# Sliding-window attention with channel mix, one core: another order of the same operations

## The chip, the cores and the metric

The kernel runs on one core of a Trainium2 chip. The metric is the device time of one execution in microseconds. Engines are named as in the profile: PE is TensorE, PEld its weight loads, DVE VectorE, ACT ScalarE, POOL GpSimd, SP SyncE. POOL and SP do almost nothing but start transfers.

## What is computed

Attention over 8 batches and 8 heads of 576 positions and 64 columns, with a window of 128 positions and a linear bias, and behind it a channel mix in which every position is mixed with the one before it:

```python
scores = scale * np.matmul(q, k.transpose(0, 1, 3, 2))
bias = slopes[:, None, None] * (-np.abs(rel).astype(np.float32))[None, :, :]
mask = (rel >= 0) & (rel < window)
scores = np.where(mask, scores + bias[None], -1000000000.0)
attn = softmax(scores)
x = np.matmul(attn, v)              # heads side by side: 8 x 576 x 512
xk = mu_k * x + (1.0 - mu_k) * x_prev
xr = mu_r * x + (1.0 - mu_r) * x_prev
k = np.maximum(xk @ w_k, 0.0)       # 512 to 1024
v = k * k @ w_v                     # 1024 to 512
out = v / (1.0 + np.exp(-(xr @ w_r)))
```

Inputs and output are float32; inside, the kernel works in bfloat16 and sums in float32.

## The kernel before

**Attention.** The work is cut into 32 pairs of heads, numbered 0 to 31; pair 4b+g is heads 2g and 2g+1 of batch b. For each pair there is a chain of operations, with these names: `tr` and `tl` (DVE transposes q and k, the large part and the tail of 64 positions, L179 and L187), `sh` (SP moves a part of q to other partitions, `qt<-qt`, L195), `score` (PE, L241 and L246, into two score banks), `exp` (ACT, L262), `mask` (DVE multiplies by the bias as a factor, L270), `av` (PE, L286, again into a score bank), `rc` and `norm` (DVE, L297 and L301, which read that bank and write xu), and then the transposition of the result. For batches 0 to 3 PE transposes (`ot`, L310) and ACT copies (`xt`, L321). For batches 4 to 7 a crossbar transpose started from SP does it (`xt` too, L315, `xt<-xu`). Batch 0 goes another way ahead of its scores: PE transposes q and k (`tq`, `tk`, `tail`), ACT and DVE copy (`pq`, `pk`, `tcopy`), and each pair is done in two parts, so that names there have a last number 0 or 1.

**Mix.** `dl` (DVE, L335) takes the difference to the position before; it is the first reader of what the transpose wrote. `ma` and `mr` scale it for the two mixes (ACT, L342, or DVE, L344), `xk` (DVE, L354) adds.

**Feed-forward.** Two batches together are a batch pair P, 0 to 3, cut into units of 256 to 512 positions. `m1.P.c.f` (PE, L366) multiplies a unit that begins at position c by a block f of w_k (in the first two blocks its first three matmuls are called `m1a`); `rl` (ACT, L372) and `kk` (ACT, L379, or DVE, L381) are the ReLU and the square; `m3` (PE, L388) and `rs` (ACT, L394) are the gate; `m2a` and `m2` (PE, L403) are the two halves of the product with w_v for 128 positions; `oo` (DVE, L410) multiplies gate and product, `st` (SP, L415) stores. In the last piece, `3.4`, `m2a`, `m2`, `oo` and `st` are done in two halves of 256 columns.

**Loads.** POOL starts them: `lql`, `lqp`, `lts` (q and k), `lvs` (v; `lvs.b.4` is its tail), `lwk`, `lwr`, `lwv` (weights). `clear.b` are DVE memsets of the places of v that no load fills (tv and vs of batch b, L487 to L489); the first `lvs` of a batch waits for it. Others at the start: `fill` (PE multiplies zeros), `sid`, `dper`, `dcopy`, `mask0`, `mcopy` (bias tables), `ms` (memsets), `c` (casts of the first q and k), `clrk`, `id8`, `tmu`, `cmu`.

**Buffers.** Four PSUM banks for matrix work ("mm"), two double banks for scores and `av` ("sa"), three buffers each for xu, the differences (mb) and rl, two for kk.

**What sets the order.** Each engine runs its instructions strictly in the order of the program. A table `ORDER` in the kernel names, for PE, ACT, DVE, POOL and SP, every operation in the order in which that engine is to run it. A loop `plan` then writes the program: it takes from each engine's list only the operation that the table has next and issues it when those that it depends on are written; its cost numbers only decide how the engines' lists are interleaved. Waits between engines follow from the data. The table has one more use: a square or a scaling whose name stands in ACT's list runs on ACT, else on DVE.

```python
for text in ORDER.values():
    line = [tuple(int(x) if x.isdigit() else x for x in w.split(".")) for w in text.split()]
    for a, o in zip(line, line[1:]):
        ops[o]["after"] = [a]
plan()
```

Of the kernel before, what the change touches and what calls it, by code (L numbers as in the profile page):

```python
# [16 lines left out]
def kernel(  # L17
# [473 lines left out]
    def clear_first():  # L491
# [5 lines left out]
            fill.8 fill.5 tq.0 fill.12 fill.6 fill.4 fill.7 fill.2 tmu tk.0 tk.3 tq.3  # L497
            tk.2 tq.2 score.0.0 score.3.0 fill.13 tail.0 tq.1 score.2.0 tk.1 fill.11
            score.3.1 av.3.0 av.0.0 score.1.0 av.2.0 ot.0.0 score.2.1 ot.3.0 av.1.0
            score.0.1 score.1.1 ot.2.0 ot.1.0 av.2.1 av.0.1 score.4 av.3.1 ot.0.1 fill.1  # L500
            av.1.1 ot.2.1 ot.3.1 score.5 ot.1.1 fill.3 av.4 fill.9 fill.0 fill.10 ot.4
            score.6 m1a.0.0.0 m1.0.0.0 m1.0.0.3 m1.0.0.2 av.5 m1.0.256.0 m1a.0.0.1
            m1.0.0.1 m1.0.256.1 m1.0.256.2 score.7 m1.0.0.4 m1.0.0.7 m1.0.0.6 ot.5 av.6
            m1.0.256.6 m3.0.1 m1.0.256.7 m3.0.2 m3.0.3 m3.0.0 m1.0.256.3 av.7 ot.6
            m1.0.0.5 m1.0.256.4 m1.0.256.5 m2a.0.0 m2a.0.3 m2a.0.1 ot.7 m2.0.0 score.8
            m2.0.3 m2.0.1 m2a.0.2 score.9 m2.0.2 m1.0.512.0 m1.0.512.2 m1.0.512.3
            score.10 m1.0.512.7 m1.0.512.1 m3.0.5 m1.0.512.6 m1.0.512.5 m1.0.768.0 av.8
            av.9 m3.0.8 ot.8 m3.0.6 score.11 m1.0.768.2 m3.0.7 m1.0.512.4 m1.0.768.3
            av.10 m1.0.768.5 av.11 m1.0.768.4 m3.0.4 ot.9 m1.0.768.1 ot.10 m2a.0.4 ot.11
            score.13 m2a.0.5 m2.0.4 m1.0.768.7 score.12 m2.0.5 m1.0.768.6 m1.1.0.0  # L510
            score.15 m1.1.0.3 m1.1.0.7 m1.1.0.6 av.12 av.13 m2a.0.8 m2.0.8 m3.1.1
            score.14 ot.13 m2a.0.6 ot.12 m1.1.0.5 m2.0.6 score.17 m1.1.0.1 m1.1.0.4
            av.14 av.15 m1.1.0.2 m2a.0.7 ot.15 m2.0.7 score.16 m3.1.3 ot.14 m2a.1.1
            m2a.1.3 score.18 m2.1.3 m2.1.1 m3.1.2 score.19 m3.1.0 m2a.1.0 av.16 m2a.1.2
            m2.1.0 m2.1.2 score.20 m1.1.512.0 m1.1.512.6 m1.1.512.7 av.19 m1.1.512.4
            m1.1.512.2 m3.1.5 av.17 av.18 m1.1.512.5 m1.1.512.3 m1.1.512.1 score.22
            m1.1.896.0 m3.1.4 m3.1.7 score.21 m3.1.6 m2a.1.4 m2a.1.5 av.20 m1.1.896.3
            m2.1.5 m2.1.4 score.23 m2a.1.6 m2.1.6 m1.1.896.1 score.24 m1.2.0.0 m1.2.0.4
            m3.2.2 m1.2.0.1 m3.1.8 av.23 m1.1.896.4 m1.1.896.2 av.22 m3.2.0 m1.1.896.7
            av.21 m1.1.896.6 m1.2.0.2 m3.2.3 score.25 m1.1.896.5 m1.2.0.3 m1.2.0.6  # L520
# [16 lines left out]
            c.0.0 mask0.6 mask0.2 mask0.0 pq.0 pk.0 pk.2 pq.3 exp.0.0 pq.2 mask0.4  # L537
            exp.3.0 exp.2.0 pq.1 exp.3.1 exp.1.0 xt.0.0 exp.2.1 xt.3.0 exp.0.1 exp.1.1
            xt.2.0 xt.1.0 exp.4.1 xt.0.1 exp.4.0 xt.3.1 ma.0.1 xt.2.1 exp.5.0 xt.1.1
            exp.5.1 ma.2.1 ma.2.0 ma.1.0 ma.3.1 ma.1.1 xt.4 exp.6.0 rl.0.0.0 rl.0.0.3  # L540
            rl.0.0.2 exp.6.1 rl.0.256.0 rl.0.0.1 kk.0.0.2 kk.0.256.0 rl.0.256.1
            rl.0.256.2 kk.0.256.1 exp.7.0 rl.0.0.4 rl.0.0.7 xt.5 rl.0.0.6 exp.7.1
            kk.0.0.7 rl.0.256.6 rl.0.256.7 rs.0.1 ma.4 rs.0.2 kk.0.0.6 rs.0.3 rl.0.256.3
            rs.0.0 kk.0.256.6 xt.6 kk.0.256.3 rl.0.0.5 mr.5 rl.0.256.4 kk.0.0.5
            rl.0.256.5 ma.6 mr.6 kk.0.256.5 xt.7 exp.8.0 exp.8.1 ma.7 exp.9.1 exp.9.0
            rl.0.512.2 rl.0.512.0 rl.0.512.3 kk.0.512.2 exp.10.1 rl.0.512.7 rl.0.512.1
            exp.10.0 kk.0.512.3 rs.0.5 kk.0.512.7 rl.0.512.6 rl.0.512.5 kk.0.512.1
            rl.0.768.0 kk.0.512.6 kk.0.768.0 xt.8 rs.0.8 rs.0.6 exp.11.0 exp.11.1
# [511 lines left out]
```

## Time and profile before

| | |
|---|---|
| median of 3 runs | 232.32 us (231.56 to 232.34) |
| the profiled execution | 232.64 us, of which the span is 230.9 |
| PE, DVE, ACT, POOL busy | 216.6, 190.2, 180.2, 72.1 us |
| granted clock of PE | 0.998 |
| moved by DMA | 32.22 MB |

The page gives busy time by engine, the span in 40 slices, the chain of work that ended last and the groups of instructions; the trace behind it gives the same for any stretch of time, with each instruction's idle time before it and what ended that. Matmuls overlap: one of 512 columns is shown with the whole time from its start to its end, though the next starts before that.

### The profile page before, as it was taken

Reading aid. Unit: us, or ns where it says so; the run is one execution under the profiler, and the core shown is the slowest. Engines: PE = TensorE matmul, PEld = TensorE weight load, DVE = VectorE, ACT = ScalarE, POOL = GpSimd, SP = SyncE. Lnnn points to the kernel's source line nnn. Section 1 sums busy time; section 2 is a strip of 40 time slices with the busy share of each in tenths; the row PEclk is TensorE's granted clock in tenths of the full one; section 3 lists DMA queues with packets and bytes.
Section 4 is the critical chain, followed back from the end, with each engine's and each line's share of the span. In section 5 each row is a group of like instructions: output and inputs, shape, how many; then the busy total and the mean of one; then the engine's idle time right before and its main releaser. Section 6 shows DMA issues by size and latency. Waiting matters only on the chain.

```text
span 230.9 us, 5631 instructions
## 1 busy us (share of the span) xinstructions
PE 216.6 (94%) x2199; PEld 127.5 (55%) x2233; DVE 190.2 (82%) x401; ACT 180.2 (78%) x334; POOL 72.1 (31%) x100
## 2 busy tenths in 40 slices
PE   7798889999999999999969899999999999999993
PEld 2445567656765565555635466464656654456542
DVE  6688999999999999999597999999897877732213
ACT  2699899998999999998698987993876778076610
POOL 8896553534567664555341000000000000000000
PEclk9999999999999999999999999999999999999999
DMA  5999999999999999999999824223411430132014
GB/s 107 180 191 142 150 203 198 210 187 192 241 163 155 197 225 196 209 218 219 162 168 140 139 82 87 77 97 77 182 30 31 125 99 0 66 119 91 0 45 183
DMA packets 83658, 32.22 MB, mean 140 GB/s; under 512 B 54568, under 2 KB 79152, under 8 KB 83632
## 3 DMA queue, kind: packets, MB, share of 16 engines
q0 software_dynamic: 61392, 16.52, 81.7%
q1 hardware_dynamic: 22240, 15.34, 27.8%
q8 instruction: 17, 0.28, 0.5%
q14 instruction: 9, 0.07, 0.1%
HBM read 33.56 MB, written 9.44 MB: 186 GB/s over the span
## 4 chain that ended last, share of the span: by engine, by line
PE 56%; DMA 15%; DVE 12%; ACT 8%; POOL 5%; issue 3%; DVEq 0%; POOLq 0%; ACTq 0%
PE ps L366 20%; PE pv L403 19%; PE pr L388 9%; DMA xt<-xu 8%; DMA tv<-in_v_dram 4%; PE sa L286 4%; ACT at L262 4%; PE sa L241 3%; DMA ql<-in_q_dram 3%; POOL vs L98 2%; DVE xm L354 2%; DVE xu L301 2%; DVE ot L410 2%; POOL ql L123 1%; ACT mb L342 1%
## 5 line engine op out<-in xcount | busy, mean ns | idle before, releaser
L262 ACT ACTIVATE at<-sa 128x1024 bf16<-128x1024 f32 x64 | 64.1, 1035 | 10.8 <-PE sa L246 10.6
L366 PE MATMUL ps<-xm,wk_sb 128*128 128x256 bf16 (+2 forms) x411 | 71.0, 313 | 0.9 <-DVE ot L410 0.5
L403 PE MATMUL pv<-wv_sb,kk 128*128 128x512 bf16 (+1 forms) x282 | 66.9, 373 | 1.7 <-DVE ot L410 0.8
L372 ACT ACTIVATE rl<-ps 128x256 bf16<-128x256 f32 (+2 forms) x104 | 46.3, 482 | 13.9 <-PE ps L366 12.5
L366 PEld LDWEIGHTS <-wk_sb 128*128 128x128 bf16 x416 | 38.8, 98 | 23.2 <-issue 0.8
L403 PEld LDWEIGHTS <-kk 128*128 128x128 bf16 x296 | 27.5, 98 | 28.6 <-issue 1.0
L270 DVE TENSOR_TENSOR at<-at,mask 128x1024 bf16<-128x1024 bf16 x56 | 37.1, 680 | 0.2
L388 PE MATMUL pr<-wr_sb,xm 128*128 128x512 bf16 x133 | 35.3, 379 | 0.7 <-issue 0.2
L410 DVE SCALAR_TENSOR_TENSOR ot<-rs,pv 128x512 f32<-128x512 bf16 (+1 forms) x37 | 24.1, 667 | 11.0 <-PE pv L403 11.0
L379 ACT ACTIVATE kk<-rl 128x256 bf16<-128x256 bf16 (+2 forms) x64 | 32.2, 523 | 0.2
L98 POOL DMA_DIRECT2D vs<-in_v_dram x32 | 28.1, 892 | 9.5 <-DMA vs<-in_v_dram 1.4
L394 ACT ACTIVATE rs<-pr 128x512 bf16<-128x512 f32 x36 | 21.8, 612 | 6.0 <-PE pr L388 6.0
L354 DVE TENSOR_TENSOR xm<-mb,xt 128x1152 bf16<-128x1152 bf16 (+3 forms) x40 | 24.6, 629 | 0.2
L342 ACT ACTIVATE mb<-mb,mu_sb 128x576 bf16<-128x576 bf16 (+2 forms) x31 | 22.3, 755 | 3.2 <-DVE mb L335 3.2
L286 PEld LDWEIGHTS <-at 128*128 128x128 bf16 x576 | 21.4, 98 | 5.8 <-issue 1.7
L381 DVE TENSOR_TENSOR kk<-rl 128x256 bf16<-128x256 bf16 (+2 forms) x40 | 13.1, 332 | 12.4 <-ACT rl L372 12.4
L301 DVE TENSOR_TENSOR xu<-sa,rc 128x640 bf16<-128x640 f32 x28 | 22.7, 816 | 0.4
L241 PE MATMUL sa<-qt,kt 32*128 32x256 bf16 x448 | 18.2, 266 | 3.3 <-DVE xu L301 1.9
L388 PEld LDWEIGHTS <-xm 128*128 128x128 bf16 x144 | 13.6, 98 | 13.3
L286 PE MATMUL sa<-vs,at 128*128 128x65 bf16 x448 | 18.8, 194 | 0.5 <-ACT at L262 0.5
L335 DVE TENSOR_TENSOR mb<-xt 128x576 bf16<-128x576 bf16 (+2 forms) x36 | 14.4, 413 | 4.1 <-DMA xt<-xu 3.8
L241 PEld LDWEIGHTS <-kt 32*128 32x128 bf16 x448 | 9.8, 92 | 13.4 <-issue 7.5
(70 smaller groups left out, 214.9 us busy)
## 6 DMA issues: line engine op xcount, KB each, us to landing
out_dram<-ot SPq DMA_DIRECT2D x35, 256.0 KB, 2.2
vs<-in_v_dram POOLq DMA_DIRECT2D x32, 128.0 KB, 10.5
ql<-in_k_dram POOLq DMA_DIRECT2D x15, 256.0 KB, 10.4
ql<-in_q_dram POOLq DMA_DIRECT2D x15, 256.0 KB, 10.1
qt<-qt SPq DMA_DIRECT2D x14, 192.0 KB, 7.3
wk_sb<-in_moe_w_k_dram POOLq DMA_DIRECT2D x2, 512.0 KB, 11.2
wv_sb<-in_moe_w_v_dram POOLq DMA_DIRECT2D x2, 512.0 KB, 13.1
tv<-in_v_dram POOLq DMA_DIRECT2D x8, 64.0 KB, 9.6
```

The costliest lines, as they stand in the source:

```text
L98: nc.gpsimd.dma_start(out=vs_buf[b % NLD][:, j, :, 0:D], in_=v[b, :, 128 * j:128 * j + 128, :].rearrange("h p d -> p h d"))
L241: nc.tensor.matmul(T["sa", it, u // 2][:, u % 2, 256 * hl:256 * hl + n], lhsT=kt[r:r + 32, h, :, par], rhs=qt[r:r + 32, h, 0:n, par], star ...
L262: nc.scalar.activation(out=to, in_=sa, func=AF.Exp, scale=float(scale))
L270: nc.vector.tensor_tensor(out=a, in0=a, in1=m, op=ALU.mult)
L286: nc.tensor.matmul(pa[:, hl, W * (t - t0):W * (t - t0) + W], lhsT=at[:, lo:lo + 128], rhs=vs[:, u, 2 * g + hl, :] if u < NF else tvb[:, 2 ...
L354: nc.vector.tensor_tensor(out=xm_buf[P % 2][:, w0:w1, o:o + c1 - c0], in0=T["mb", it][:, w0:w1, c0:c1], in1=x_of(it, c0 - 1, c1 - 1)[:, No ...
L366: nc.tensor.matmul(ps[:, 0:c1 - c0], lhsT=wk_sb[:, po, 128 * fo:128 * fo + 128], rhs=xk[:, po, c0:c1], start=(po == 0), stop=(po == NPO - 1))
L372: nc.scalar.activation(out=rl[:, 0:c1 - c0], in_=T.pop(("ps", P, c0, fo))[:, 0:c1 - c0], func=AF.Relu, scale=RELU_SCALE)
L379: nc.scalar.activation(out=out_, in_=in_, func=AF.Square)
L388: nc.tensor.matmul(pr, lhsT=T["xr", P][:, po, 128 * c:128 * c + 128], rhs=wr_sb[:, po], start=(po == 0), stop=(po == NPO - 1))
L403: nc.tensor.matmul(pv[:, m0:m1], lhsT=kk[:, fo, o:o + 128], rhs=wv_sb[:, fo, m0:m1], start=(fo == 0), stop=(fo == NFO - 1))
L410: nc.vector.scalar_tensor_tensor(out=T["ot", P, c][:, m0:m1], in0=T["rs", P, c][:, m0:m1], scalar=1.0, in1=T["pv", P, c][:, m0:m1], op0=AL ...
```

## The change

All five lists of `ORDER` are replaced; nothing else in the kernel differs, but for one line more in the file. PE, POOL and SP have the same operations as before (332, 94 and 71 names). 41 squares, scalings and copies go from DVE to ACT and 36 the other way. The lists differ in nearly every line; of them the diff is shown for the places of SP's list about the crossbar transposes of batch 4, and for the end of PE's list:

```diff
         "PE": """
...
-            m1.3.896.6 m1.3.896.5 m1.3.896.7 m3.3.7 m2a.3.6 m1.3.896.4 m2.3.6 m3.3.4
-            m3.3.8 m2a.3.8 m2a.3.5 m2a.3.7 m2.3.8 m2.3.5 m2.3.7 m2a.3.4.0 m2.3.4.0
-            m2a.3.4.1 m2.3.4.1
...
+            m2a.3.8 m2a.3.5 m2a.3.7 m2.3.8 m2a.3.6 m2.3.5 m2.3.7 m2.3.6 m3.3.4 m2a.3.4.0
+            m2.3.4.0 m2a.3.4.1 m2.3.4.1
...
         "SP": """
...
-            st.0.7 st.1.1 st.1.3 xt.16 st.1.0 st.1.2 xt.19 xt.17 xt.18 sh.6.0 xt.20
...
+            st.0.7 st.1.3 st.1.1 xt.16 st.1.2 st.1.0 xt.19 xt.17 sh.6.0 xt.18 sh.6.1
+            st.1.5 xt.20 sh.7.1 st.1.6 st.1.4 xt.21 xt.22 st.1.8 sh.7.0 xt.23 st.1.7
```

In PE's list the operations between `score.24` and the first matmul of batch pair 2, `m1.2.0.0`, are none before; now they are `m2.1.4 m3.1.8 m3.1.7 av.22 m2a.1.8 av.21 m2.1.8`.

**DVE at the first crossbar transpose.** DVE before, from `norm.19` on (xu is what a crossbar transpose reads, and `mb<-xt` is the difference `dl`, which reads what it wrote; the first such row is `dl.16`, and the two pairs of rows behind it are `rc` and `norm` of 17 and 18):

```order
L297 RECIPROCAL rc<-sa 128x10
L301 TENSOR_TENSOR xu<-sa,rc 128x2x5x64
L270 TENSOR_TENSOR at_83<-at_83,mask 128x2x512
L187 STREAM_TRANSPOSE qt_89<-kl_87 32x8x2x32
L335 TENSOR_TENSOR mb_99<-xt_94 128x576
L297 RECIPROCAL rc<-sa 128x10
L301 TENSOR_TENSOR xu<-sa,rc 128x2x5x64
L297 RECIPROCAL rc<-sa 128x10
L301 TENSOR_TENSOR xu<-sa,rc 128x2x5x64
```

The same place now, from `norm.19` on:

```order
L297 RECIPROCAL rc<-sa 128x10
L301 TENSOR_TENSOR xu<-sa,rc 128x2x5x64
L270 TENSOR_TENSOR at_83<-at_83,mask 128x2x512
L381 TENSOR_TENSOR kk<-rl 128x384
L270 TENSOR_TENSOR at_83<-at_83,mask 128x2x512
L297 RECIPROCAL rc<-sa 128x10
L301 TENSOR_TENSOR xu<-sa,rc 128x2x5x64
L179 STREAM_TRANSPOSE qt_89<-ql_79 128x4x4x32
L270 TENSOR_TENSOR at_81<-at_81,mask 128x2x512
L179 STREAM_TRANSPOSE kt_85<-ql_79 128x4x4x32
L335 TENSOR_TENSOR mb_99<-xt_94 128x576
```

Before the difference stand now also a square, a mask, `rc` and `norm` of 17 and the two large transposes of batch 6; the first of these is what the move `sh.6.0` waits for, and it stood behind `dl.16` before. Between `norm.16` and this piece stand ten operations now (one difference, one scaling, three mixes, three masks, two products), where there were eight (one scaling, two mixes, three masks, two products).

**DVE at the start.** Before, ahead of the first cast of q and k (tv_91 and vs_76 are batch 0's buffers of v, tv_92 and vs_77 batch 1's):

```order
L454 COPY dist<-dist 128x128
L487 MEMSET tv_91 64x520
L488 MEMSET tv_91 128x8
L489 MEMSET vs_76 128x32
L493 MEMSET xm_97 128x4x32
L487 MEMSET tv_92 64x520
L488 MEMSET tv_92 128x8
L489 MEMSET vs_77 128x32
L128 CAST xm_97<-xm_97 128x2x4x64 x2
```

Now, the piece that ends with batch 1's memsets, just ahead of the first `rc` and `norm`:

```order
L947 MEMSET xt_95 128x4x16
L187 STREAM_TRANSPOSE qt_90<-kl_88 32x8x2x32
L187 STREAM_TRANSPOSE kl_88<-kl_88 32x8x2x32
L487 MEMSET tv_92 64x520
L488 MEMSET tv_92 128x8
L489 MEMSET vs_77 128x32
L297 RECIPROCAL rc<-pa 128x2x2
L301 TENSOR_TENSOR xu<-pa,rc 128x2x2x64
```

Batch 1's memsets (`clear.1`) stood among the first instructions of DVE and stand now behind the copies of batch 0, the large transpose `tr.1.0.0`, `clear.2`, `ms` and the small transposes of batch 1. POOL's loads of batch 1's v stand at the same place of POOL's list in both, with one exchange among the five.

More of the change, by code (lines that the diff above doesn't have):

```diff
@@ L619 @@
+            rc.31 norm.31 ma.28 kk.3.0.6 rc.29 norm.29 dl.30 xk.28 kk.3.0.4 ma.30 mr.30
+            oo.2.8 dl.29 mr.29 xk.30 dl.31 oo.2.7 oo.3.0 xk.31 ma.29 xk.29 oo.3.2 oo.3.1
+            oo.3.3 kk.3.512.0 kk.3.896.0 kk.3.512.5 kk.3.896.2 kk.3.512.7 kk.3.512.2
+            kk.3.512.4 kk.3.896.3 kk.3.896.5 oo.3.8 oo.3.5 oo.3.7 oo.3.6 oo.3.4.0
+            oo.3.4.1
         """,
         "POOL": """
-            lql.0.1.1 place lts.1.1 lql.0.1.0 lql.1.0.0 lts.0.1 lts.0.0 lts.1.0 lqp.1.0
-            lqp.1.1 lvs.0.1 lvs.0.0 lql.1.1.0 lvs.0.3 lql.1.0.1 lvs.0.4 lvs.0.2 lvs.1.0
@@ L641 @@
+            xt.24 xt.25 xt.27 st.2.2 st.2.3 st.2.1 st.2.0 xt.26 st.2.4 st.2.6 st.2.5
+            xt.28 xt.30 xt.31 xt.29 st.2.8 st.2.7 st.3.0 st.3.2 st.3.1 st.3.3 st.3.8
+            st.3.5 st.3.7 st.3.6 st.3.4.0 st.3.4.1
         """,
```

255 lines of the change are left out of this document (125 added, 130 removed).

## Prediction

> **What bounds the kernel now.** I read the page first: busy shares, then the slices.
>
> ```profile
> span 230.9 us, 5631 instructions
> PE 216.6 (94%) x2199; PEld 127.5 (55%) x2233; DVE 190.2 (82%) x401; ACT 180.2 (78%) x334; POOL 72.1 (31%) x100
> ...
> PE   7798889999999999999969899999999999999993
> ...
> DVE  6688999999999999999597999999897877732213
> ```
>
> TensorE (PE) is busy 94% of the span, and DVE too is full as far as slice 19. So a change of order can win only where PE stands still. The table of windows of 10 us shows where.
>
> ```profile
> core 0: us, PE busy (x) PEld busy (x) DVE busy (x) ACT busy (x) POOL busy (x), PEclk, DMA share, GB/s
> ...
> 20.00:30.00 10.00, 8.23 (x147) 5.71 (x148) 9.11 (x29) 9.04 (x17) 5.77 (x9) 1.00 2.64 149
> ...
> 50.00:60.00 10.00, 9.89 (x119) 6.71 (x120) 9.93 (x18) 9.28 (x18) 4.98 (x7) 1.00 1.93 213
> ...
> 110.00:120.00 10.00, 7.95 (x102) 5.16 (x101) 7.32 (x13) 7.66 (x17) 4.85 (x6) 1.00 1.62 168
> 120.00:130.00 10.00, 9.63 (x97) 5.21 (x96) 8.78 (x19) 9.09 (x14) 0.69 (x1) 1.00 1.87 124
> 130.00:140.00 10.00, 9.20 (x112) 6.09 (x115) 9.40 (x17) 8.34 (x17) 0.00 (x0) 1.00 0.34 110
> 140.00:150.00 10.00, 9.95 (x95) 5.04 (x97) 9.93 (x19) 9.26 (x17) 0.00 (x0) 1.00 0.41 85
> ```
>
> An undisturbed window holds 9.9 us of PE, and the clock stays at 1.00. There are three holes: 20 to 30, 110 to 140, and the end. The table of waits (104 to 135) and DVE's timeline explain the middle one (a row of waits ends with us, times, longest; a row of the timeline begins with start and us, and ends with the idle time before it).
>
> ```profile
> PE sa L241 <- DVE xu L301: 1.9, 2, 1.2
> PE ps L366 <- DVE ot L410: 0.5, 1, 0.5
> PE sa L241 <- ACT at L262: 0.3, 1, 0.3
> PE sa L241 <- DMA qt<-qt: 0.2, 1, 0.2
> ...
> 104.99 0.82 DVE L301 TENSOR_TENSOR xu<-sa,rc 128x640 bf16<-128x640 f32 x1
> ...
> 112.15 0.70 DVE L187 STREAM_TRANSPOSE qt<-kl 32x512 f32<-32x512 f32 x1
> 115.35 0.46 DVE L335 TENSOR_TENSOR mb<-xt 128x576 bf16<-128x576 bf16 x1 [2.49 <-DMA xt<-xu]
> ...
> 130.19 0.40 PE L241 MATMUL sa<-qt,kt 32*128 32x256 bf16 x8 [0.24 <-DMA qt<-qt]
> ```
>
> DVE stops for 2.49 us because it stands at `dl.16`, the first reader of a crossbar transpose. Behind it are queued `rc.17`, `norm.17`, `rc.18` and `norm.18`, which free the score banks; PE's `score.22` waits for those (the 1.9 us). The last of the four waits is that of `score.24` for the move of q, `sh.6.0`; it starts at 130.19. The chain of waits gives what the two transposes on it take:
>
> ```profile
> 105.88 9.44 DMA xt<-xu
> ...
> 116.82 7.92 DMA xt<-xu
> ...
> 152.14 0.55 PE sa L286 x18
> ...
> 219.81 5.20 PE pv L403 x24
> ```
>
> **The change, part by part.** The sum is made against the profiled execution: 232.64 us, of which the span is 230.9 and 1.74 lie around it. That is 0.32 above the median of the runs shown, 232.32. PE's operations are the same 332; some squares and scalings change between ACT and DVE, about as many either way (DVE loses 4 net).
>
> *A, the middle.* I count what DVE does between `norm.16` and `dl.16`, with the durations of the groups:
>
> ```profile
> L270 DVE TENSOR_TENSOR at<-at,mask 128x1024 bf16<-128x1024 bf16 x56 | 37.1, 680 | 0.2
> L410 DVE SCALAR_TENSOR_TENSOR ot<-rs,pv 128x512 f32<-128x512 bf16 x35 | 23.4, 681 | 10.3 <-PE pv L403 10.3
> L301 DVE TENSOR_TENSOR xu<-sa,rc 128x640 bf16<-128x640 f32 x28 | 22.7, 816 | 0.4
> L354 DVE TENSOR_TENSOR xm<-mb,xt 128x1152 bf16<-128x1152 bf16 x28 | 20.6, 752 | 0.2
> L179 DVE STREAM_TRANSPOSE qt<-ql 128x512 f32<-128x512 f32 x14 | 15.4, 1098 | 0.0
> ```
>
> Before: four masks (2.72), two products (1.36), two mixes (1.50), one normalisation (0.82), one small transpose (0.70) and two short rows (estimated at 0.6 together) are 7.7, less than 9.44: it stalls. (From the end of `norm.16`, 105.8, to that of the row at 112.15 they really took 7.0: rows overlap a little, 0.91 of their durations.) Now: six masks (4.08), three mixes (2.26), two products (1.36), two normalisations (1.63), two large transposes (2.20) and five short rows (1.6) are 13.1, which covers 9.44. `dl.17` has 25 rows between it and `norm.17` in place of 10, and `dl.18`, `dl.19` some 12 us each. `sh.6.0` starts behind `tr.6.0.0`, which now comes before `dl.16`, so the move has some 10 us before `score.24`. These waits go.
>
> What they are worth on PE: its idle rows here are 1.9 + 0.5 + 0.3 + 0.2 = 2.9. A busy row of PE ends with the latency of its last matmul (24 matmuls of L403 take 5.20, 0.216 each, while one lasts 0.379 by its group), so each of the five waits hides 0.16 more: 3.7.
>
> What is late next: `m1.2.0.0`, the first matmul of the third batch pair, needs the mix `xk.18`. From `dl.16` to the end of `xk.18` DVE now has 33 instructions (four differences, six scalings, five masks, four mixes, four transposes, three products and so on), 19.0 us by durations and 17.3 at the pace of 0.91. `norm.16` stands 1.4 us of DVE's work earlier than before, so `xk.18` ends at 105.8 - 1.4 + 12.0 + 17.3 = 133.7. PE's work ahead of `score.24` is the same to +0.4, and four of the five waits (3.1 of the 3.7) lay before it: 130.2 + 0.4 - 3.1 = 127.5. Between it and `m1.2.0.0` there stood nothing; now there stand 20 matmuls of 512 columns (4.3) and two `av` (0.55 each by the row of L286; 5.4 together): PE is there at 132.9 and waits 0.8. With 0.1 for smaller waits part A is -3.7 + 0.9 = **-2.8** (between 0 and -3.7).
>
> *B, 140 to 185.* `m1.2.512.0` needs the mixes of batch 5:
>
> ```profile
> 159.33 1.43 DVE L354 TENSOR_TENSOR xm<-mb,xt 128x1152 bf16<-128x1152 bf16 x2
> ...
> 161.89 0.82 PE L366 MATMUL ps<-xm,wk_sb 128*128 128x384 bf16 x4
> ```
>
> They end at 160.8 and it starts at 161.9: 1.1 us to spare. In the new order DVE has 0.7 us more ahead of the last of them and PE 0.6 less ahead of the matmul, so 0.2 wait, and 0.3 I leave for `score.30` behind `norm.26`. `dl.26` now follows `norm.26` closely, so DVE waits there, but the mix behind it has room. **+0.5** (0 to +2).
>
> *C, the start.* The first feed-forward matmul is bound by a load:
>
> ```profile
> L366 PE MATMUL ps<-xm,wk_sb x411: 271/326/390, 32.0 to 216.9; 128*128 128x256 bf16 x65, 128*128 128x384 bf16 x43, 128*128 128x512 bf16 x29
> L470 POOL DMA_DIRECT2D wk_sb<-in_moe_w_k_dram x2: 740/744/747, 21.9 to 23.5; - x2
> ...
> DMA to landing us min/median/max: 10.1/11.2/12.3
> ...
> 15.48 0.49 DVE L487 MEMSET tv<- 64x520 bf16 x1
> ...
> 14.17 4.41 POOL L98 DMA_DIRECT2D vs<-in_v_dram  x5
> ...
> DMA to landing us min/median/max: 5.7/8.1/10.5
> ```
>
> `lwk.0` is issued at 21.9 and lands 10.1 later, at 32.0, when that matmul starts. All its forerunners are the same loads, so a faster start of PE wins nothing. But `clear.1`, the memset of tv_92 for which POOL's `lvs.1` loads wait, stood early on DVE. Now it stands behind all that stood ahead of `clear.2`, which began at 15.48 (`tr.1.0.0`, the copies, both small transposes), and behind `pk.2` (0.7, as the copy `pk.3`), `clear.2` itself (0.7) and six memsets (0.5): it begins near 17.4 and ends near 18.0. So POOL stands from 15.0 to 18.0, where it had issued `lvs.1.0` (the second of the five) at 15.0. Loads already issued go on landing to 14.2 + 8.1 = 22.3. An unhindered load takes 5.7 at least: 23.7 in place of 15.0 + 8.1 = 23.1. **+0.5** (0 to +4).
>
> *D, 30 to 107.* PE, DVE and ACT are all full. ACT now has `ma.7` (about 0.8 by its neighbours) ahead of `exp.8.0`, which sets free the banks for `score.9`:
>
> ```profile
> 49.83 1.02 ACT L262 ACTIVATE at<-sa 128x1024 bf16<-128x1024 f32 x1 [0.46 <-PE sa L246]
> ```
>
> Of the 0.8, 0.46 fall into ACT's idle time there. Elsewhere the shifts of the order are under 0.8 us. **+0.4** (0 to +1.3).
>
> *E, the end.*
>
> ```profile
> 225.43 1.61 DVE L410 SCALAR_TENSOR_TENSOR ot<-rs,pv 128x512 f32<-128x512 bf16 x3 [0.58 <-PE pv L403]
> 227.10 0.60 PE L403 MATMUL pv<-wv_sb,kk 128*128 128x256 bf16 x4 [0.80 <-DVE ot L410]
> ```
>
> PE's last four matmuls waited 0.80 for `oo.3.4.0`, queued behind `oo.3.7` and `oo.3.8`. Now `m3.3.4` (four matmuls, 0.86) stands between the last `m2` and the final ones, so DVE has worked off its queue. Of 0.80, 0.1 to 0.2 remain: **-0.7** (0 to -0.8).
>
> Sum: 232.64 - 2.8 + 0.5 + 0.5 + 0.4 - 0.7 = **230.5**.
>
> **The rivals.** *1, the wait moves.* In 140 to 150 DVE is at 9.93, as full as PE, so what PE wins can be given back at the next mix that it needs (`xk.18`, `xk.23`). For it: terms A and B leave under 1 us between the two engines twice. Against: DVE loses its own idle time too, 2.49 of it in one row. If 1.8 us of the 2.8 come back: 232.3.
>
> *2, the loads run dry (slower).* If DVE reaches `clear.1` not at 18.0 but at 21.5, the first `lvs.1` lands at 27.2 in place of 23.1, and with it `lwk.0` and everything behind: 230.5 - 0.5 + 4.1 = 234.1. It decides from 20.0 on, where a shift of 2.6 eats the gain. For it: on that way DVE's rows wait for copies of PE's transposes three times and for ACT's masks once. Against: 2 us of margin in my sum.
>
> *3, the transposes hinder each other.* In the new order `xt.19`, `xt.17` and `sh.6.0` are issued close together. If two in flight took twice 9.44, 18.9, `dl.19`, with 12 us of DVE's work between it and `norm.19`, would stall for 6.9. If 3 of these lie beside PE's stock of 5.4 ahead of `m1.2.0.0`, 3.9 are added: 234.4. Against:
>
> ```profile
> 116.82 2.54 SPq L315 DMA_TRANSPOSE xt<-xu  x2
> ```
>
> `xt.17` and `xt.18` were issued within these 2.54 us, and `xt.17` took 7.92, less than `xt.16` alone. The Trainium skill (DMA: Bandwidth & Descriptors, "Issuing engines are not separate DMA queues") says that DMAs of all issuing engines run on the same 16 DMA engines and interleave. By that rule rival 3 would come about; the trace shows no such doubling for two transposes.
>
> *4, all waits go* and B to D cost nothing: 232.64 - 3.7 - 0.7 = 228.2.
>
> **How the numbers follow.** Forecast 0.58, rival 1 0.22, rival 2 0.11, rival 3 0.04, rival 4 0.05. The predicted time is 230.5. The range is 228.4 to 233.4: it takes in the ends of A and rival 1 and leaves out most of rivals 2, 3 and 4. Half a per cent, 1.2 us, is about what a measurement of this kernel can tell from no change, so faster means under 231.2: the forecast and rival 4, 0.63. Within: rival 1, 0.22. Slower: rivals 2 and 3, 0.15.
>
> **What would show it.** A: no wait of DVE for `xt` between 104 and 128, PE at 9.6 or more in the windows of 110 to 130, `score.24` near 127.5, `m1.2.0.0` near 133.7. B: a wait of PE's L366 or L241 for DVE's `xm` or `xu` near 155 to 170 of under 1 us. C: the first `wk_sb` matmul at 32 to 33, and POOL idle for 3 us before an `lvs.1`. E: the last wait of PE under 0.3. It is wrong if that first matmul is later than 34, or if PE's idle time reappears between 130 and 165.

## The result and the profile after

| | before | changed |
|---|---|---|
| median of the runs beside each other | 232.33 us (231.56 to 233.06, 4 runs) | 229.92 us (228.65 to 230.11, 4 runs) |
| ratio, with 95% interval | | 0.9885 (0.9837 to 0.9933) |
| the profiled execution; its span | 232.64 us; 230.9 | 230.11 us; 228.3 |

The changed kernel is 1.1% faster; 230.5 was forecast. The page of the changed kernel has the same work in its busy shares. In its 40 slices, counted from 0, PE's hole in slice 20 (115.5 to 121.2 us before) is gone, and the one at the start is deeper (slices of 5.7 us):

```profile
span 228.3 us, 5615 instructions
PE 215.6 (94%) x2199; PEld 127.4 (56%) x2233; DVE 188.7 (83%) x396; ACT 182.9 (80%) x339; POOL 72.1 (32%) x100
...
PE   7897779999999999999999999999999999999993
...
DVE  7399799999999999999999999999957883951141
```

The table of windows of 10 us, with the busy time of each engine, says the same in numbers: PE 6.72 in 20 to 30, where it had 8.23, and 9.95, 9.74 and 9.95 in the three windows from 110, where it had 7.95, 9.63 and 9.20.

```profile
20.00:30.00 10.00, 6.72 (x135) 4.99 (x135) 8.15 (x25) 8.45 (x16) 7.34 (x11) 1.00 2.79 144
...
110.00:120.00 10.00, 9.95 (x121) 6.55 (x120) 9.83 (x18) 9.16 (x21) 4.19 (x6) 1.00 1.60 176
120.00:130.00 10.00, 9.74 (x123) 6.43 (x125) 9.72 (x20) 9.54 (x19) 0.59 (x1) 1.00 2.28 117
130.00:140.00 10.00, 9.95 (x94) 5.14 (x93) 9.72 (x19) 7.67 (x13) 0.00 (x0) 1.00 1.23 158
```

To see where the time went, I set each PE operation's start against the PE work that stands before it in its list, and subtracted the one kernel's difference from the other's. The result is how late the changed kernel is at a point of equal work done (us):

| at | changed minus before |
|---|---|
| the first wk_sb matmul (33.4 against 32.0) | +1.4 |
| around 100 | +1.3 |
| around 130 | -2.2 |
| 170 to 220 | -2.3 |
| the last four matmuls | -2.5 |

The change therefore loses 1.4 us at the start, gains 3.5 between 105 and 130, keeps everything to the end, and gains another 0.2 on the last matmuls. From 104 on, DVE's timeline has no idle time at `dl.16` (first of the rows below) and none at `dl.19`, `dl.17` and `dl.18`, `mb<-xt` too, to 131 (start, duration; a row with idle time would end with it):

```profile
117.04 0.44 DVE L335 TENSOR_TENSOR mb<-xt 128x576 bf16<-128x576 bf16 x1
...
124.37 0.45 DVE L335 TENSOR_TENSOR mb<-xt 128x576 bf16<-128x576 bf16 x1
...
129.25 0.45 DVE L335 TENSOR_TENSOR mb<-xt 128x576 bf16<-128x576 bf16 x1
```

PE's timeline has `score.24` at 129.00 and the first matmul of batch pair 2 at 135.00, without idle time before it:

```profile
129.00 0.40 PE L241 MATMUL sa<-qt,kt 32*128 32x256 bf16 x8
...
134.35 0.81 PE L403 MATMUL pv<-wv_sb,kk 128*128 128x512 bf16 x3
135.00 1.89 PE L366 MATMUL ps<-xm,wk_sb 128*128 128x512 bf16 x8
```

One execution of the same kernel differs from the next by more here than in the runs shown with the prediction: in the experiments the kernel before took 230.3 to 235.5. So times decide only what is above 0.5%; below that the waits in the profiles decide. The profiled executions of x4 and x9, of 370.8 and 446.1 us, are not read and not in the medians given here.

### The profile page after: what moved, and what is told of

It is laid out like the page before. It is cut to its first block, busy times and chain, and to the rows that moved or that the text cites. A ratio compares the mean times of both kernels' runs of the same rounds, so it can differ in the third digit from the quotient of the medians.

```text
span 228.3 us, 5615 instructions
## 1 busy us (share of the span) xinstructions
PE 215.6 (94%) x2199; PEld 127.4 (56%) x2233; DVE 188.7 (83%) x396; ACT 182.9 (80%) x339; POOL 72.1 (32%) x100
## 4 chain that ended last, share of the span: by engine, by line
PE 84%; DVE 6%; DMA 4%; ACT 2%; issue 2%; POOL 1%; DVEq 0%; ACTq 0%
PE ps L366 28%; PE pv L403 27%; PE pr L388 14%; PE sa L286 7%; PE sa L241 6%; DMA vs<-in_v_dram 4%; PE xp L310 1%; ACT mask L463 1%; POOL vs L98 1%; PE sa L246 1%; DVE sid L457 1%; ACT L463 1%; DVE kt L179 0%; DVE qt L179 0%; DVE tv L487 0%
## 5 line engine op out<-in xcount | busy, mean ns | idle before, releaser
L403 PE MATMUL pv<-wv_sb,kk 128*128 128x512 bf16 (+1 forms) x280 | 65.6, 373 | 1.8 <-issue 0.6
L372 ACT ACTIVATE rl<-ps 128x256 bf16<-128x256 f32 (+2 forms) x104 | 46.5, 479 | 11.7 <-PE ps L366 10.8
L379 ACT ACTIVATE kk<-rl 128x256 bf16<-128x256 bf16 (+2 forms) x70 | 34.5, 524 | 0.2
L342 ACT ACTIVATE mb<-mb,mu_sb 128x576 bf16<-128x576 bf16 (+2 forms) x30 | 21.4, 750 | 6.3 <-DVE mb L335 6.3
L381 DVE TENSOR_TENSOR kk<-rl 128x256 bf16<-128x256 bf16 (+2 forms) x34 | 10.7, 320 | 15.5 <-ACT rl L372 15.5
L301 DVE TENSOR_TENSOR xu<-sa,rc 128x640 bf16<-128x640 f32 x28 | 22.7, 818 | 0.4
L335 DVE TENSOR_TENSOR mb<-xt 128x576 bf16<-128x576 bf16 (+2 forms) x36 | 14.5, 414 | 3.2 <-DMA xt<-xu 3.1
L179 DVE STREAM_TRANSPOSE qt<-ql 128x512 f32<-128x512 f32 x14 | 15.4, 1102 | 0.1
```

Source lines behind the costliest of these rows:

```text
L372: nc.scalar.activation(out=rl[:, 0:c1 - c0], in_=T.pop(("ps", P, c0, fo))[:, 0:c1 - c0], func=AF.Relu, scale=RELU_SCALE)
L379: nc.scalar.activation(out=out_, in_=in_, func=AF.Square)
L403: nc.tensor.matmul(pv[:, m0:m1], lhsT=kk[:, fo, o:o + 128], rhs=wv_sb[:, fo, m0:m1], start=(fo == 0), stop=(fo == NFO - 1))
```

## The experiments

Two questions: which of the moved rows made the middle faster, and what made the start slower. Times stand against the kernel before on the same chip.

**x1: `clear.1` back to the start.** On the changed kernel.

```diff
-            clrk sid c.0.0 dper clear0 id8 dcopy c.0.1 pk.3 pk.2 tr.1.0.0 tcopy.0 cmu
-            mcopy clear.2 ms tl.1.0 tl.1.1 clear.1 rc.2.0 norm.2.0 rc.0.0 norm.0.0
+            clrk sid c.0.0 dper clear0 id8 dcopy c.0.1 clear.1 pk.3 pk.2 tr.1.0.0 tcopy.0 cmu
+            mcopy clear.2 ms tl.1.0 tl.1.1 rc.2.0 norm.2.0 rc.0.0 norm.0.0
```

> The changed kernel with clear.1 on DVE moved back to the start, right behind c.0.1, where DVE had 1.94 us idle. Theory (the pause of POOL made the loads late): POOL's idle 2.60 us ahead of the first load lvs.1 goes, that load is issued near 15.5 in place of 18.06, lwk.0 lands near 32.0 in place of 32.94, the first wk_sb matmul starts at 32.0 to 32.5 in place of 33.4, and the time falls by 0.9 to 1.4 from 229.9, to about 228.8. Rival a (DVE's and PE's own chain sets the start): the loads land earlier, but score.6 and the first wk_sb matmul stay at 32.8 and 33.4; 229.9. Rival b (the gain is given back in the middle): the start gains 1.2, but m1.2.0.0, for which xk.18 was only 0.9 early, waits for DVE; 229.4.

229.18 us, ratio 0.9859 (0.9813 to 0.9904). The interval overlaps the changed kernel's, so the times alone do not tell the two apart. POOL's pause ahead of `lvs.1` is gone and the first wk_sb matmul starts at 32.5; hardly anything of it is lost later. That looks like the theory, until one asks when the loads became earlier: `lvs.0.2`, which is issued ahead of the place where the pause was (13.9, and 14.5 in the changed kernel), landed at 22.2 already, against 23.6. The pause cannot have caused that. Nor is it sure that the edit did: in x8, which has the same start, `lvs.0.2` landed at 23.4 and the first wk_sb matmul started at 32.8. x7, x10 and x11 look further.

**x2: in the kernel before, `dl.16` alone late.**

```diff
-            rc.19 norm.19 mask.18.1 tl.6.0 dl.16 rc.17 norm.17 rc.18 norm.18 tl.6.1
-            tr.6.0.1 mask.20.1 mask.22.1 kk.1.512.3 mask.20.0 tr.6.0.0 kk.1.512.5 dl.19
+            rc.19 norm.19 mask.18.1 tl.6.0 rc.17 norm.17 rc.18 norm.18 tl.6.1
+            tr.6.0.1 dl.16 mask.20.1 mask.22.1 kk.1.512.3 mask.20.0 tr.6.0.0 kk.1.512.5 dl.19
```

> The kernel before with one row of DVE moved: dl.16 behind norm.18, tl.6.1 and tr.6.0.1. Theory (the wait for the crossbar transpose at the head of DVE's queue held the score banks): DVE's idle 2.49 us at dl.16 goes, norm.17 ends near 114 in place of 116.8, PE's wait of 1.9 us at score.22 goes, and the time falls by 1.9 to 2.5 from 232.3, to 229.8 to 230.4. Rival a (DVE is the bound, so the wait moves to the next mix): PE's 1.9 reappears at m1.2.0.0 or at another matmul before 145; 232.0 to 232.3. Rival b (the new order of PE, not that of DVE, removed the stall): score.22 still waits over 1 us; above 231.5.

233.58 us, ratio 1.0040 (1.0006 to 1.0075): not faster at all. The theory missed; rival a has the right course (the wait reappears before 145) with a cause that I had not named. DVE's wait at `dl.16` did go, `norm.17` ended at 114.3, and `score.22` waited no more. But PE then stood 2.68 us at `m3.1.4`. ACT's timeline shows why; before first, then x2:

```profile
112.97 0.60 ACT L394 ACTIVATE rs<-pr 128x512 bf16<-128x512 f32 x1
115.84 0.78 ACT L342 ACTIVATE mb<-mb,mu_sb 128x576 bf16<-128x576 bf16 x1 [2.27 <-DVE mb L335]
...
117.35 1.23 ACT L372 ACTIVATE rl<-ps 128x384 bf16<-128x384 f32 x3
```

```profile
113.03 0.60 ACT L394 ACTIVATE rs<-pr 128x512 bf16<-128x512 f32 x1
117.44 0.77 ACT L342 ACTIVATE mb<-mb,mu_sb 128x576 bf16<-128x576 bf16 x1 [3.81 <-DVE mb L335]
...
118.94 1.23 ACT L372 ACTIVATE rl<-ps 128x384 bf16<-128x384 f32 x3
```

`ma.16` (L342) scales what `dl.16` writes and stands on ACT right behind `rs.1.5`. So the transpose was awaited at the head of two queues. Behind `ma.16` stand three ReLUs (L372) that free PE's banks; with `dl.16` later they came 1.6 later.

**x3: in the changed kernel, `dl.16` early.**

```diff
-            xk.12 mr.14 mask.19.0 xk.15 xk.14 mask.17.1 mask.19.1 oo.1.2 oo.1.0 rc.19
+            xk.12 mr.14 mask.19.0 xk.15 xk.14 mask.17.1 mask.19.1 oo.1.2 oo.1.0 dl.16 rc.19
...
-            tr.6.0.1 dl.16 rc.18 norm.18 mask.20.0 tl.6.1 tr.6.1.0 oo.1.5 tl.6.0 ma.16
+            tr.6.0.1 rc.18 norm.18 mask.20.0 tl.6.1 tr.6.1.0 oo.1.5 tl.6.0 ma.16
```

> The changed kernel with dl.16 moved forward on DVE, ahead of rc.19, where DVE is at 111.1 while xt.16 lands at 113.3. Theory (DVE is full until 134, so a wait at the head of its queue costs PE all but the slack behind it): DVE waits 2.2 us there; score.22 has 4.4 us of slack behind norm.17 now and does not wait, but score.23 has only 0.3 behind norm.20 and m1.2.0.0 0.9 behind xk.18: PE loses 1.3 to 1.9 there, and the time is 231.2 to 231.8. Rival a (the place of dl.16 matters little now, because PE's list has more work between av.18 and score.22): 229.9 to 230.3. Rival b (the stall returns where it was): PE idles 1.5 or more at score.22.

231.95 us, ratio 0.9975 (0.9929 to 1.0022). DVE's timeline, and PE's:

```profile
113.23 0.46 DVE L335 TENSOR_TENSOR mb<-xt 128x576 bf16<-128x576 bf16 x1 [2.27 <-DMA xt<-xu]
```

```profile
116.21 0.63 PE L286 MATMUL sa<-vs,at 128*128 128x65 bf16 x15 [1.87 <-DVE at L270]
```

The size is the theory's (2.27 on DVE, 1.87 on PE, 1.9 at the end by equal work), the place is not: PE lost it at `av.18`, which needs `mask.18.0`, one of the rows queued behind `dl.16`. I had looked only at the score banks. A single reader of a transpose, ten operations too early, takes back most of what the change gained.

**x6: in the changed kernel, `ma.16` from DVE back to its place on ACT.**

```diff
-            kk.1.512.2 rs.1.5 kk.1.512.6 rl.1.512.3 rl.1.512.5 kk.1.512.3 rl.1.512.7
+            kk.1.512.2 rs.1.5 ma.16 kk.1.512.6 rl.1.512.3 rl.1.512.5 kk.1.512.3 rl.1.512.7
...
-            tr.6.0.1 dl.16 rc.18 norm.18 mask.20.0 tl.6.1 tr.6.1.0 oo.1.5 tl.6.0 ma.16
+            tr.6.0.1 dl.16 rc.18 norm.18 mask.20.0 tl.6.1 tr.6.1.0 oo.1.5 tl.6.0
```

> The changed kernel with one scaling, ma.16, put back from DVE to the place that it had on ACT, right behind rs.1.5. Theory (two queues): ACT stands from 114.9 to 117.5 for dl.16, 2.6 us, the ReLUs behind it free PE's banks late, PE waits 1.5 to 2.5 at an L366 or L388 matmul between 115 and 120, and the time is 231.3 to 232.3, all of the change's gain lost. Rival (ACT has the slack, and DVE's queue alone counted): PE's loss is under 0.5 and the time within 0.4 of 229.9.

234.00 us, ratio 1.0102 (1.0053 to 1.0151), more than expected. The waits are as expected (ACT's timeline, and PE's):

```profile
117.32 0.77 ACT L342 ACTIVATE mb<-mb,mu_sb 128x576 bf16<-128x576 bf16 x1 [2.60 <-DVE mb L335]
```

```profile
118.93 0.81 PE L366 MATMUL ps<-xm,wk_sb 128*128 128x384 bf16 x4 [2.39 <-ACT rl L372]
```

The profiled execution was 232.85, 2.7 above the changed kernel's, and that is what the waits explain; why the median lies another 1.2 higher is open. One scaling of 0.8 us, put early into ACT's list, costs all of the gain, since the engine stands in front of it until `dl.16` has run. `ma.16` late on ACT was not tried in the changed kernel.

**x5: in the kernel before, `dl.16` and `ma.16` late.** The edit of x2, and on ACT

```diff
-            rl.1.512.7 kk.1.512.6 rl.1.512.2 rl.1.512.4 kk.1.512.7 rs.1.5 ma.16
-            kk.1.512.4 kk.1.512.2 rl.1.512.3 rl.1.512.5 rl.1.512.1 exp.22.1 exp.22.0
+            rl.1.512.7 kk.1.512.6 rl.1.512.2 rl.1.512.4 kk.1.512.7 rs.1.5
+            kk.1.512.4 kk.1.512.2 rl.1.512.3 rl.1.512.5 rl.1.512.1 exp.22.1 exp.22.0 ma.16
```

> The kernel before with dl.16 late on DVE as in x2_before_dl16_late, and ma.16, which reads it, late on ACT too, behind exp.22.0. Theory (the transpose was awaited at the head of two queues: dl.16 on DVE, and ma.16 on ACT, where the ReLUs that free PE's banks are queued behind it, so both must move): ACT no longer stands for 2.3 us behind rs.1.5, PE idles under 0.5 between 112 and 125 instead of 1.9 (2.7 in x2_before_dl16_late), and the time is 229.9 to 230.6, as the changed kernel's. Rival a (the new order of PE is what helps): PE still waits over 1.5 there, 232 or more. Rival b (the wait moves to m1.2.0.0 or to score.24): PE idles at these by 1 or more, 231.2 to 232.

231.62 us, ratio 0.9991 (0.9965 to 1.0017). The expected 229.9 to 230.6 did not come. Both waits at the first transpose are gone and PE does not stand between 111 and 124. Then DVE stands at the next reader, `dl.17`, as long as it had stood at `dl.16`, and PE at `score.23`, for `exp.21.1` behind `ma.17` on ACT (PE's table of waits from 100 to 150, and DVE's timeline):

```profile
PE sa L241 <- ACT at L262: 2.0, 1, 2.0
```

```profile
124.63 0.46 DVE L335 TENSOR_TENSOR mb<-xt 128x576 bf16<-128x576 bf16 x1 [2.53 <-DMA xt<-xu]
```

**x9 and x12: `dl.17` late too.** The edit of x5, and the readers of the second transpose behind `norm.20` and `exp.21.1`:

```diff
-            mr.19 dl.17 xk.16 rc.20 mr.17 norm.20 dl.18 oo.1.5 xk.17 mr.18 oo.1.4 xk.18
+            mr.19 xk.16 rc.20 norm.20 dl.17 mr.17 dl.18 oo.1.5 xk.17 mr.18 oo.1.4 xk.18
...
-            kk.1.512.1 rs.1.4 rl.1.896.0 exp.21.0 mr.16 rs.1.7 ma.19 ma.17 exp.21.1
+            kk.1.512.1 rs.1.4 rl.1.896.0 exp.21.0 mr.16 rs.1.7 ma.19 exp.21.1 ma.17
```

> The kernel before with the readers of two crossbar transposes late: dl.16 and ma.16 as in x5_before_dl16_ma16_late, and dl.17 and mr.17 on DVE behind norm.20, ma.17 on ACT behind exp.21.1. Theory (every reader at the head of a queue must move; in x5 the wait only went from dl.16 to dl.17, behind which rc.20, norm.20 and exp.21.1 stood, which score.23 needs): DVE's wait for a transpose ahead of norm.20 goes, PE idles under 0.6 between 112 and 130 where x5 had 2.0 at score.23, and the time is 229.6 to 230.4, with PE's list of before unchanged. Rival (PE's old list is late anyway: score.23, score.24 and m1.2.0.0 wait for the next reader or for the move of q): PE idles 1.2 or more between 126 and 136, and the time is 231 to 232.

233.47 us, ratio 1.0028 (0.9978 to 1.0078). x12 is the same kernel, run again for its profile.

> The kernel of x9_before_dl16_dl17_late again, for its profile, which was disturbed: where does PE stand between 112 and 140, when the readers of the first two transposes stand late on DVE and ACT and PE's list is that of before? Theory of two queues alone: PE idles under 0.6 there. What the times of x9 (no gain over before) suggest instead: the wait has gone on to the next reader or to a matmul that PE's old list has early, so that PE idles 1.5 to 2.5 in all at score.23, score.24 (move of q) or m1.2.0.0 (xk.18), and DVE waits 1 or more at dl.17 or dl.18; time 231 to 233.

232.32 us, ratio 0.9989 (0.9929 to 1.0049). PE's waits in 104 to 150, and its timeline:

```profile
PE sa L241 <- DMA qt<-qt: 2.1, 1, 2.1
PE pv L403 <- ACT rs L394: 0.8, 1, 0.8
```

```profile
130.44 0.40 PE L241 MATMUL sa<-qt,kt 32*128 32x256 bf16 x8 [2.14 <-DMA qt<-qt]
```

`score.22` starts at 115.66 (116.85 before) and `score.23` at 124.50 (127.00), so PE is up to 2.5 ahead. Then it stands at `score.24` until 130.44: the move `sh.6.0`, issued at 120.62 behind the late `tr.6.0.0`, had landed at 130.40. In the kernel before, the same wait was the row of 0.24 of the prediction, and `score.24` started at 130.19. The fourth step, `tr.6.0.0` and the move early as in the changed kernel (move issued at 115.97), was not tried in the kernel before. DVE, too, still stands for transposes, at `dl.19`, `dl.17` and `dl.18`, for 2.5 in all.

**x7: in the kernel before, `clear.1` late.**

```diff
-            sid dper ms dcopy clear0 clear.1 c.0.1 id8 clrk cmu pk.3 tr.1.0.0 tl.1.1
-            tl.1.0 tcopy.0 mcopy clear.2 pk.1 rc.3.0 rc.0.0 norm.3.0 norm.0.0 tr.1.1.0
+            sid dper ms dcopy clear0 c.0.1 id8 clrk cmu pk.3 tr.1.0.0 tl.1.1
+            tl.1.0 tcopy.0 mcopy clear.2 clear.1 pk.1 rc.3.0 rc.0.0 norm.3.0 norm.0.0 tr.1.1.0
```

> The kernel before with clear.1 on DVE moved from the start to behind clear.2, so that it begins near 16 in place of 6.1. Theory (the memset holds back POOL's loads): POOL idles about 2 us before lvs.1.0, that load is issued near 17.3 in place of 15.0, the first wk_sb matmul starts 0.7 to 1.4 later than 32.0, and the time rises by as much, to 232.9 to 233.7. Rival (the eight loads in flight limit POOL anyway, since it idled 1.7 at 19.3): the first wk_sb matmul moves by under 0.4; 232.2 to 232.6.

231.82 us, ratio 0.9998 (0.9969 to 1.0027); the first wk_sb matmul started at 31.4, earlier than before. POOL stood 1.70 and issued `lvs.1.0` at 16.89 in place of 15.03, yet it landed at 22.8 in place of 23.2. The loads of v, by the tile's view and POOL's timeline, before first (the row of times to landing is for `lvs.0.2` and the four of batch 1 behind it; of these four alone the median is 8.9) and then x7 (the four):

```profile
20.97 0.76 POOL L123 DMA_DIRECT2D ql<-in_k_dram  x1 [1.71 <-DMA ql<-in_k_dram]
...
DMA to landing us min/median/max: 8.0/8.3/10.5
```

```profile
16.89 3.50 POOL L98 DMA_DIRECT2D vs<-in_v_dram  x4 [1.70 <-DVE vs L489]
...
DMA to landing us min/median/max: 5.9/7.0/8.4
```

What is issued later lands in less time: the loads stand in line behind one another, and this pause of POOL cost nothing. POOL had also stood 1.71 before, a little later (the row at 20.97). In x7 that wait is gone, and `lwk.0` is issued at 21.8 as before (21.9). So the theory falls, and the rival is right as to the pause. That everything landed earlier in x7 is not the edit's doing as far as shown: `lvs.0.2`, ahead of the pause, landed at 21.5 in place of 22.2 too.

**x10 and x11: the first 26 loads of POOL exchanged.** x10 is the changed kernel with POOL's order of before, x11 the reverse:

```diff
-            place lql.0.1.0 lql.0.1.1 lql.1.0.0 lts.1.1 lts.0.1 lts.0.0 lts.1.0 lqp.1.1
-            lqp.1.0 lvs.0.1 lvs.0.0 lql.1.1.0 lql.1.0.1 lvs.0.3 lvs.0.4 lvs.0.2 lvs.1.3
-            lvs.1.2 lvs.1.4 lvs.1.0 lvs.1.1 lql.1.1.1 lwk.0 lql.2.0.0 lwk.1 lwr
+            lql.0.1.1 place lts.1.1 lql.0.1.0 lql.1.0.0 lts.0.1 lts.0.0 lts.1.0 lqp.1.0
+            lqp.1.1 lvs.0.1 lvs.0.0 lql.1.1.0 lvs.0.3 lql.1.0.1 lvs.0.4 lvs.0.2 lvs.1.0
+            lvs.1.2 lvs.1.3 lvs.1.1 lvs.1.4 lql.1.1.1 lwk.0 lql.2.0.0 lwk.1 lwr
```

> The changed kernel with the first 26 loads of POOL in the order of before, nothing else changed (clear.1 stays late on DVE, POOL still pauses ahead of the batch 1 loads). Theory (the order of the first loads sets the start: landings follow one another without a gap, as x7_before_clear1_late showed, so a pause of POOL costs nothing, but what lands first does): lvs.0.2 lands near 22.2 in place of 23.6, lwk.0 near 32.0 in place of 32.9, the first wk_sb matmul starts at 32.0 to 32.6, and the time is 228.8 to 229.4. Rival (the lists of PE, DVE and ACT at the start set it): the first wk_sb matmul stays at 33.1 or later, 229.7 to 230.2.

229.54 us, ratio 0.9891 (0.9832 to 0.9950). POOL stood even longer, 3.4, and still `lvs.1.0` landed 1.0 behind `lvs.0.2` (22.2 and 23.2), as before:

```profile
  DVE rc L297: 3.4, 1
...
DMA to landing us min/median/max: 4.3/5.1/6.7
```

(The row names `rc`; the memset's last two instructions are recorded beside it.) The first wk_sb matmul started at 32.8, against 33.4, 33.1 and 33.3 in the three kernels with the changed start (changed, x3, x6). `lwk.0`, issued at 23.8, had landed at 32.6, where the four kernels with the start of before (before, x2, x5, x12) have 31.8 to 32.4. So about half of what was expected came at this matmul, and by the times nothing (the changed kernel's ratio is 0.9885). PE waits for no load there, yet it is still 0.4 to 0.8 late.

> The kernel before with the first 26 loads of POOL in the order of the changed kernel, nothing else changed. Theory (the order of the first loads sets the start): lvs.0.2 lands near 23.2 in place of 22.2, the first wk_sb matmul starts at 32.7 to 33.4 in place of 32.0, and the time is 232.9 to 233.6. Rival (the lists of PE, DVE and ACT at the start set it): the first wk_sb matmul stays at 32.3 or earlier, and the time is 232.2 within 0.4.

233.34 us, ratio 1.0018 (0.9977 to 1.0059). The first wk_sb matmul started at 33.2, against 32.0, 32.3, 32.0 and 32.4 in those four: 1.0 late, most of what the change lost there. The time alone is not told from the kernel before. PE's timeline shows where. It stands in `av.0.1`, batch 0's second half, until the last load of batch 0's v, `lvs.0.2`, has landed; before, changed kernel and x11:

```profile
22.25 0.40 PE L286 MATMUL pa<-vs,at 128*128 128x65 bf16 x8 [0.60 <-DMA vs<-in_v_dram]
```

```profile
23.67 0.40 PE L286 MATMUL pa<-vs,at 128*128 128x65 bf16 x8 [1.94 <-DMA vs<-in_v_dram]
```

```profile
22.76 0.50 PE L286 MATMUL pa<-vs,at 128*128 128x65 bf16 x8 [1.66 <-DMA vs<-in_v_dram]
```

`lvs.0.2` landed at 22.2, 23.6 and 22.7. It is issued ahead of POOL's pause. In x10 it landed at 22.2 and PE had no wait there. Executions with the same start scatter by up to 1.2 here (x1 and x8), so all twelve profiles count: the six with POOL's order of before (before, x2, x5, x7, x10, x12) have `lvs.0.2` at 21.5 to 22.5 and the first wk_sb matmul at 31.4 to 32.8, the six with the new order (changed, x1, x3, x6, x8, x11) at 22.2 to 23.6 and 32.5 to 33.4. The means differ by about 0.9 in both. (Of the first six only x10 has the changed lists of the other engines, of the second all but x11.)

**x4 and x8: a bank of its own for the last half.** In the changed kernel; x8 has the edit of x1 too.

```diff
-        if half == 0 and m0 == 0:
-            T["pv", P, c] = p_mm.tile([128, 512], FP32, tag="mm", name="pv")
-        pv = T["pv", P, c]
+        if half == 0:
+            T["pv", P, c, m0] = p_mm.tile([128, 512], FP32, tag="mm", name="pv")
+        pv = T["pv", P, c, m0]
...
```

(Cut: `oo`, and the list of what each operation uses, name the new bank in the same way.)

> The changed kernel with a PSUM bank of its own for the second half (256 columns) of the last piece, m2a.3.4.1 and m2.3.4.1, which shared one with the first half. Theory (the last wait of PE is no longer one for DVE's queue but comes from the shared bank: oo.3.4.0 reads it behind m2a.3.4.1, and m2.3.4.1 writes it behind oo.3.4.0): PE's wait of 0.57 before its last four matmuls goes, and the time falls by 0.4 to 0.6, to about 229.4. Rival (DVE is late anyway, or the new bank is not yet free): a wait of 0.3 or more stays and the time is the same within 0.2.

> The changed kernel with both edits at once: clear.1 early on DVE (x1_clear1_early) and a bank of its own for the second half of the last piece (x4_after_own_bank). Theory: the start gains 0.7 to 1.0 as in x1_clear1_early, and PE's last wait, 0.57 for oo.3.4.0, goes; the time is 228.5 to 228.9. Rival (the shared bank is not what PE waits for at the end): a wait of 0.3 or more stays before the last four matmuls, and the time is that of x1_clear1_early, 229.2.

x4: 229.23 us (3 runs), ratio 0.9858 (0.9807 to 0.9910). x8: 228.82 us, ratio 0.9883 (0.9850 to 0.9916). The changed kernel's end first, then x8's:

```profile
222.52 1.47 PE L403 MATMUL pv<-wv_sb,kk 128*128 128x256 bf16 x12
...
224.09 0.42 DVE L410 SCALAR_TENSOR_TENSOR ot<-rs,pv 128x256 f32<-128x256 bf16 x1 [1.54 <-PE pv L403]
224.56 0.60 PE L403 MATMUL pv<-wv_sb,kk 128*128 128x256 bf16 x4 [0.57 <-DVE ot L410]
```

```profile
222.08 1.91 PE L403 MATMUL pv<-wv_sb,kk 128*128 128x256 bf16 x16
```

With one bank, `oo.3.4.0` starts only when all twelve matmuls have ended, the first four of the other half among them, and the last four wait for `oo.3.4.0`. With two banks all sixteen run in one piece, and the wait of 0.57 is gone. x8 has the lowest median of all, but its interval and the changed kernel's overlap: the profile shows that the wait went; that x8 is faster than the changed kernel the times do not show.

## Why the prediction came out, point by point

- **A, the middle, -2.8: right in mechanism, -3.5 measured.** All five waits went, as summed to -3.7 (2.9 in rows and 0.16 behind each). The 0.9 that I took off did not come: `m1.2.0.0` did not wait for `xk.18`. The mix ended at 134.12, near the 133.7 of my count of DVE's rows; PE came later than counted, `score.24` at 129.0 in place of 127.5, and the start's loss of 1.4, which stood in neither count, accounts for nearly all of that. (Two counts on the way were off: between `norm.17` and `dl.17` stand 26 rows in place of 12, not 25 in place of 10; nothing hangs on it.) Whether the 0.9 would have come with the start of before is not shown; x1, 0.7 to 0.8 earlier than the changed kernel throughout, has no such wait either.
- What A's text had incomplete is **why** the waits went. I named DVE's queue. x2, x3, x5, x6 and x12 show a row of three: the readers of the first transpose on DVE and on ACT, those of the second, and the move of q; each hid the next. A sum of idle rows is only worth its full value if all that stands behind them moves as well; here it did. By the times, none of the steps x2, x5 and x9 gained anything in the kernel before. No run sets the changed lists of DVE, ACT and SP beside PE's list of before, or the reverse. So how much of the gain PE's own new order brings is not shown; x3 and x6 show that it is not enough by itself.
- **C, the start, +0.5: the mechanism failed, and the size.** The step "POOL stands from 15.0 to 18.0" came nearly true (2.60 idle, to 18.06), but no load is shown to be late by it: behind pauses of 1.7 (x7) and 3.4 (x10) the first load of batch 1's v landed at 22.8 and 23.2, and at 23.1 to 23.5 in the four kernels with the start of before. Some lateness of `lwk.0` is not excluded (32.6 in x10, 31.8 to 32.4 in those four). "An unhindered load takes 5.7 at least" took the fastest of eight loads that stood in line for one that stood in none; x10 has 4.3. The loss was 1.4 (the matmul at 33.4, outside the 32 to 33 that I had named), and PE falls behind earlier, at `av.0.1`, where it waits for `lvs.0.2`. The order of the first loads by itself is worth 1.0 at the first wk_sb matmul with the lists of before (x11), and 0.3 to 0.6 with the changed ones (x10). I had set that order aside, and described it wrongly: the five loads of batch 1's v are not one exchange apart but stand in another order altogether, and nine of the seventeen places ahead of them differ too. Open is which of these moves makes `lvs.0.2` late, why the first wk_sb matmul came 0.3 to 0.8 earlier with `clear.1` early (x1 and x8), and what makes up the 0.4 to 0.8 that x10 keeps. One candidate, not tried: `c.0.0`, a cast of the first q and k, also went from ACT to DVE, which the count of 36 moves leaves out.
- **B, +0.5, and D, +0.4: both near 0.** The lateness stays near -2.3 from 130 to 220, and moves from 1.4 to 1.3 between 35 and 100. These two were reserves for waits that I could not exclude. At `m1.2.512.0` (158.90; mixes ended at 158.18) there is none.
- **E, the end, -0.7: -0.2.** "Of 0.80, 0.1 to 0.2 remain" failed: 0.57 remained. DVE's queue was empty, as forecast, but there was a second cause of 0.57 under the first, the bank that both halves share (x8).
- The forecast came near the time in part by luck, because errors in size cancelled: C cost 0.9 more and E gave 0.5 less than forecast, A, B and D together gave 1.8 more (0.7, 0.6 and 0.5).
- **Rival 1** (the wait moves to DVE) did not happen in the changed kernel. In the kernel before, x2, x5 and x12 show waits that move, though to a ReLU, an `exp` and the move of q, and not to a mix. **Rival 2** (loads run dry) did not happen, and x7 and x10 speak against its mechanism as far as their pauses of 1.7 and 3.4 go. **Rival 3**: `xt.19`, `xt.17`, `sh.6.0` and `xt.18` took longer in the changed kernel (9.2 to 11.2, against 7.5 to 9.0 before), not twice as long, and the rows of DVE between them covered it. That they took longer because they were in flight together is not shown: with the same order of the four, x10 has 8.2 to 9.2 and x3 7.5 to 9.6. The Trainium skill (DMA: Bandwidth & Descriptors, "Issuing engines are not separate DMA queues") says that the DMAs of all issuing engines run on the same 16 DMA engines; no run here separates what that costs. **Rival 4** was right as to A, B and D, and wrong at C and E.

## What to carry to other kernels

When a transfer is awaited at the head of an engine's queue, list all readers, on every engine, and what stands behind each of them: moving one reader gained nothing here, nor did moving more of them while the next wait stood right behind (x2, x5, x12), and putting one back cost most or all of the gain (x3, x6). Before pricing a pause of the engine that issues loads, ask whether the loads stand in line: if the time to landing falls by as much as the issue is later, as it did for the loads of v in x7 and x10, the pause costs nothing there. And look at more than one execution: the landings at the start scattered by about a microsecond between executions with the same start. Last, a wait that is named for a queue can have a second cause beneath it (0.57 of 0.80 here).

## What was unexpected of the hardware

- The time from issue to landing of the same four v loads fell from 8.9 (before) to 7.0 (x7) and 5.1 (x10; medians) when they were issued 1.86 and 3.85 later, with the landings moved by under 0.5.
- In the changed kernel, the crossbar transposes `xt.19`, `xt.17` and `xt.18` took 9.2 to 11.2 us while loads ran, and those issued after the last load had landed at 136.0 took 2.6 to 4.1 (`xt.24`, issued at 152.76, landed at 155.36), as far as the trace has their landings. No run varies the loads alone, so that they are the cause is not shown. The view of the transposes of the changed kernel:

```profile
L315 SPq DMA_TRANSPOSE xt<-xu x16: 1200/1212/1928, 105.5 to 188.4; - x16
...
DMA to landing us min/median/max: 2.6/3.9/11.2
```
